# Low parts of MLP tiles behind the next additions, an earlier split of the staged w3, and im0's low part one block ahead

## The chip, the cores and the metric

One core of a Trainium2 chip runs the whole program. The metric is the device time of one execution in microseconds. The engines are TensorE (PE, matmuls), VectorE (DVE), ScalarE (ACT), GpSimd (POOL) and SyncE (SP, which issues every DMA of this kernel). Each engine works through its own list of instructions in order and waits on semaphores for the others.

## What is computed

Two layers, each an FNet mixing block followed by an MLP block, over x of 2048 x 512 in float32. Cut from the reference:

```python
a = einsum("bsd,ed->bse", x, dft_hid_re); b = einsum("bsd,ed->bse", x, dft_hid_im)
y = einsum("ts,bse->bte", dft_seq_re, a) - einsum("ts,bse->bte", dft_seq_im, b)
# MLP block
h = gelu(layernorm(x) @ w1)            # 512 x 512, then quarters of h shifted by +1, -1, +2, -2 rows
x1 = x + shifted(h) @ w2               # 512 x 512
out = x1 + gelu(layernorm(x1) @ w3) @ w4   # 512 x 1376, 1376 x 512
```

Each layer is x + mixing(layernorm(x)), then x + MLP(layernorm(x)).

## The kernel before

Every float32 operand is **split** into a high part (a rounded copy, made by ACT) and a low part (the operand minus the high part, made by DVE, one TENSOR_TENSOR). A product of two operands is three matmuls (`mm3`, lines 283 to 285: high x high, high x low, low x high). So the third matmul of each product needs the low part of the left operand, the second that of the right one. The sequence of 2048 rows is worked on in four chunks of 512.

**Mixing, per chunk.** `x_phase` and `y_phase` build four half products of the sequence transform over eight blocks k each; matrices come from memory by DMA into `raw` tiles, are combined and split into a `ring` of four tiles and used by PE in that order. At the end of `y_phase` the four results (re0, im0, re1, im1, in tiles rr) are split too: `high(im0)` on ACT, `low(im0)` on DVE (line 506, helper line 409). The blocks end in the order (6, by1), (7, by1), (6, by0), (7, by0). In the last chunk the hidden transform (`hid`) follows at once, and its first product reads im0; in the others im0 is read some blocks later in the next chunk. `stream()`, called before each block, emits the splits of the ring tiles that come next, line 246 among them.

**The spatial-shift part.** `by_pairs` runs 32 slots: chunk c has slots 8c to 8c + 7, four `shifted` blocks (x w1, gelu, shift; the result split into tiles rg) and four `mixed` blocks (rg x w2, added to the input on DVE from PSUM, line 688). Other work is hung into these slots by a table: `D(slot, f)` emits f ahead of the slot's own eviction, `A(slot, f)` behind it. There stand the statistics of the next layernorm (`u_stats`), the transposes that turn chunks by way of DRAM (`turn_out` stores a turned chunk, `bring` loads it back), sums of two chunks' blocks (tiles b11 to b22 and t1 to t4, "bt"), and the first loads and splits of w3 and w4.

**The MLP in pairs.** Chunks 0 and 1 (layer 0), and both pairs of chunks (layer 1), go through x w3 two at a time with seven products in place of eight (a scheme of sums and differences of blocks). NF = 11 tiles of 128 hidden units make one single tile and five pairs p = 0 to 4. In layer 0 the w3 pair is loaded raw into one buffer, `staged` (line 869), its four sums are made on DVE (`w3_sums`, line 448, in w3bf), its three groups are split (`w3_highs` on ACT line 887, `w3_lows` on DVE line 893), and the finished w3 is stored to DRAM (`w3_keep`, line 896) for layer 1, which loads it ready made. The w4 tiles are split (`w4_high` line 852, `w4_low` line 856) and stored likewise. There are two w3 buffers (w3b 203 and 205) and six of w4 (w4r).

A pair is, in order of PE: products "11" (bank b1), "t2" (b6), "t1" (b5), "21" (b2), "t3" (b7), then two `w4_part` blocks of the pair before (12 matmuls each, one in p = 0), "t4" (b4) and "22" (b3). A product is six matmuls. The banks come round in fours, so each product overwrites the bank of the fourth one ahead of it: "21" needs "22" of the previous pair to be read, "22" needs "t1" to be read. DVE adds the products up in u, v, x and y (line 448): x and y read the bank of "t1" (b5), x also that of "22". After u and v stand gelu (ACT, line 643, into a tmp tile), the high part (line 646) and the low part (line 647) of h4, which `w4_part` reads a pair later; x and y are kept as gelu in hc and split later. `at_point(0)` to `at_point(5)` emit the preparation of the next pair's weights; `one()` emits one piece of other work from a list (bg), such as `finish` (the layernorm of a chunk) and its transposes. Only layer 0 prepares weights; layer 1 has the pairs with loads alone.

What sets the order of all this is the code's own order: each engine executes its list as written.

## Time and profile before

| | |
|---|---|
| median of 3 runs | 1480.0 us (1479.96 to 1481.51) |
| the profiled execution | 1479.5 us, its span 1477.6 us |
| PE busy | 1455.5 us, 99% of the span |
| DVE busy | 1121.9 us, 76% |
| ACT busy | 715.5 us, 48% |
| DMA | 277 MB, mean 188 GB/s |
| the chain that ended last | PE 80%, DVE 11%, DMA 4%, ACT 2% |

How to read the lines below. Every time is in microseconds from the span's start. A line of the timeline is: start, duration, engine, line of the code, operation, what is written from what, shape, count; in brackets the idle time of the engine before it and what ended that. In a view of waits a line reads: who waits, for whom, the total, the number of times, the longest. A row of stretches gives, after the window, its length and then the busy time (and count) of PE, PE's weight load, DVE, ACT and POOL, the granted PE clock, the share of DMA and its rate in GB/s. A row of DMA issues ends with the size of one and the median time from issue to landing.

### The profile page before, as it was taken

The page shows a single profiled execution, that of the slowest core. Times are in us where ns is not written, and L with a number is a line of the kernel's source. Part 1 is how long each engine was busy: PE and PEld are TensorE (multiplying, and loading weights), DVE is VectorE, ACT ScalarE, POOL GpSimd, SP SyncE. Part 2 cuts the span into 40 slices and gives each one's busy share as a digit, 9 for nine tenths or more (in the row PEclk, how much of TensorE's full clock was granted, in tenths as well). Part 3 has the DMA queues.
Part 4 walks back from the last instruction along what each step waited for, and adds up shares of the span by engine and source line. Part 5 has one row for each costly group of instructions (what it writes and reads, how often), then busy time and mean ns, then how long its engine had stood idle before and what let it go on. Part 6 is the DMA issues. An engine that isn't in the chain of part 4 may idle for free.

```text
span 1477.6 us, 17320 instructions
## 1 busy us (share of the span) xinstructions
PE 1455.5 (99%) x6374; PEld 1190.9 (81%) x6374; DVE 1121.9 (76%) x1558; ACT 715.5 (48%) x953; POOL 86.8 (6%) x111
## 2 busy tenths in 40 slices
PE   9999999999999998999999999999999999999998
PEld 7888888888878776888887888888887788888887
DVE  6876987988868866757989979979888688646443
ACT  5563454444557544435545544644445675333231
POOL 2100000000001000001100000000000010000000
PEclk9999999999999999999999999999999999999999
DMA  6426556566546657862445466565665467768444
GB/s 234 137 87 210 191 187 214 181 196 236 190 127 166 205 176 252 289 208 73 141 130 185 153 204 191 194 219 178 194 225 179 131 166 276 222 213 300 157 133 157
DMA packets 110500, 277.17 MB, mean 188 GB/s; under 512 B 8400, under 2 KB 37072, under 8 KB 108496
## 3 DMA queue, kind: packets, MB, share of 16 engines
q1 hardware_dynamic: 110416, 276.07, 57.1%
q8 instruction: 50, 0.82, 0.2%
q14 instruction: 34, 0.28, 0.1%
HBM read 231.21 MB, written 44.83 MB: 187 GB/s over the span
## 4 chain that ended last, share of the span: by engine, by line
PE 80%; DVE 11%; DMA 4%; ACT 2%; issue 2%; SPq 0%; POOL 0%; DVEq 0%; ACTq 0%
PE psd L285 9%; PE psd L283 8%; PE psd L284 8%; PE psa L283 7%; PE psa L285 7%; PE psa L284 7%; PE psc L285 6%; PE psc L283 6%; PE psc L284 6%; PE psb L285 6%; PE psb L283 6%; PE psb L284 6%; DVE ring L246 2%; DMA raw<-in_ws 2%; DMA staged<-in_w 1%
## 5 line engine op out<-in xcount | busy, mean ns | idle before, releaser
L230 ACT CAST ring<-raw 128x1024 fp32r<-128x1024 f32 (+1 forms) x153 | 156.5, 1029 | 124.2 <-PE psd L285 49.3
L246 DVE TENSOR_TENSOR ring<-raw,ring 128x1024 fp32r<-128x1024 f32 (+1 forms) x153 | 181.7, 1191 | 33.5 <-ACT ring L230 31.5
L283 PE MATMUL psd<-ring,rr 128*128 128x512 f32 x208 | 80.9, 389 | 0.0
L284 PE MATMUL psd<-ring,rr 128*128 128x512 f32 x208 | 80.9, 389 | 0.0
L285 PE MATMUL psd<-ring,rr 128*128 128x512 f32 x208 | 80.9, 389 | 0.0
L647 DVE TENSOR_TENSOR h<-tmp,h 128x512 fp32r<-128x512 f32 x53 | 36.7, 692 | 52.5 <-ACT h L646 50.7
L323 POOL TENSOR_TENSOR rs<-ve,mhalf 128x4 f32<-128x4 f32 x16 | 27.8, 1739 | 612.7 <-DVE nm L322 612.7
L302 POOL TENSOR_TENSOR rs<-ve,mhalf 128x2 f32<-128x2 f32 (+1 forms) x33 | 34.4, 1042 | 423.1 <-DVE nb L301 415.3
L331 ACT ACTIVATE tmp<-xs,nb,rs 128x512 f32<-128x512 f32 x58 | 44.7, 809 | 19.0 <-POOL nb L303 19.0
L284 PE MATMUL psc<-ring,ay 128*128 128x512 f32 x128 | 50.0, 391 | 1.3 <-DVE ring L246 1.2
L237 ACT CAST ring<-ring2f 128x1024 fp32r<-128x1024 f32 x28 | 29.6, 1057 | 44.1 <-DVE ring2f L236 44.1
L283 PE MATMUL psc<-ring,ay 128*128 128x512 f32 x128 | 49.9, 390 | 0.3 <-ACT rr11f L473 0.3
L284 PE MATMUL psb<-ring,ay 128*128 128x512 f32 x128 | 49.9, 390 | 0.2 <-DVE ring L246 0.2
L285 PE MATMUL psc<-ring,ay 128*128 128x512 f32 x128 | 49.8, 389 | 0.0
L285 PE MATMUL psb<-ring,ay 128*128 128x512 f32 x128 | 49.8, 389 | 0.0
L283 PE MATMUL psb<-ring,ay 128*128 128x512 f32 x128 | 49.8, 389 | 0.0
L237 ACT CAST ring<-ring0f 128x1024 fp32r<-128x1024 f32 x28 | 29.6, 1058 | 41.6 <-DVE ring0f L236 41.6
L246 DVE TENSOR_TENSOR ring<-ring1f,ring 128x1024 fp32r<-128x1024 f32 (+1 forms) x50 | 49.2, 983 | 0.6 <-ACT ring L233 0.4
L246 DVE TENSOR_TENSOR ring<-ring3f,ring 128x1024 fp32r<-128x1024 f32 (+1 forms) x50 | 49.1, 982 | 0.2
L285 PE MATMUL psa<-ring,ay 128*128 128x512 f32 x126 | 49.0, 389 | 0.0
L283 PE MATMUL psd<-ring,ay 128*128 128x512 f32 x126 | 49.0, 389 | 0.0
L284 PE MATMUL psa<-ring,ay 128*128 128x512 f32 x126 | 49.0, 389 | 0.0
(480 smaller groups left out, 4369.3 us busy)
## 6 DMA issues: line engine op xcount, KB each, us to landing
raw<-in_ws SPq DMA_DIRECT2D x183, 512.0 KB, 4.9
raw<-in_hs SPq DMA_DIRECT2D x56, 512.0 KB, 3.6
w4r<-w4d SPq DMA_DIRECT2D x55, 512.0 KB, 4.1
w3b<-w3d SPq DMA_DIRECT2D x10, 1792.0 KB, 7.7
raw<-in_w SPq DMA_DIRECT2D x26, 512.0 KB, 3.6
w3d<-w3b SPq DMA_DIRECT2D x5, 1792.0 KB, 6.8
x1d<-tmp SPq DMA_DIRECT2D x12, 512.0 KB, 6.5
xs<-x1d SPq DMA_DIRECT2D x12, 512.0 KB, 6.6
```

The costliest lines, as they stand in the source:

```text
L230: nc.scalar.copy(dest[:, a:b, 0], r[0][:, a:b])
L237: nc.scalar.copy(dest[:, :, 0], lo)
L246: nc.vector.tensor_tensor(lo, src, hi.bitcast(F32), op=ALU.subtract)
L283: nc.tensor.matmul(o, lh, rh, start=first, stop=False)
L284: nc.tensor.matmul(o, lh, rl, start=False, stop=False)
L285: nc.tensor.matmul(o, ll, rh, start=False, stop=last)
L302: nc.gpsimd.tensor_tensor(rs[:, :n], ve[:, :n], mhalf[:, 0, :n], op=ALU.pow)
L323: nc.gpsimd.tensor_tensor(rs, ve, mhalf[:, :, :2], op=ALU.pow)
L331: nc.scalar.activation(o, s, AF.Identity, bias=mr[2], scale=mr[1])
L647: nc.vector.tensor_tensor(dst[:, 1], g, dst[:, 0].bitcast(F32), op=ALU.subtract)
```

## The change

It edits five places, and moves instructions on DVE, ACT and SP; PE's list stays as it was.

1. In `y_phase`, `low(im0)` is emitted before block (6, by0)'s matmuls instead of (7, by0)'s.
2. In each pair of the MLP (both layers), the low part of u's gelu tile goes behind the additions into v and y, that of v's behind the addition of "22" into x.
3. In layer 0's pairs, the low parts of w3's second and third group come at point 2, followed by the load of the next staged w3; the low part of the first group and the store come at point 4; the w4 high parts move to point 3.
4. In layer 0, the first w3 pair is loaded at slot 19, and split in slots 23 to 25 in place of slots 29 to 31 and the start of the MLP; the second is loaded at slot 25. The first low part of w4 is made at slot 31.
5. In layer 0, the statistics `u_stats(2, 2)` move from slot 25 to the list of other work behind the MLP's first block.

```diff
@@ y_phase: the last chunk step for block k == NP - 2, "by0"
-                if last:
+                if k == NP - 2:
                     low(im0)
@@ splitting a gelu tile
+    def split_low(dst, g):
+        nc.vector.tensor_tensor(dst[:, 1], g, dst[:, 0].bitcast(F32), op=ALU.subtract)
+
     def split(dst, g, copy=nc.vector.tensor_copy):
         copy(dst[:, 0], g)
-        nc.vector.tensor_tensor(dst[:, 1], g, dst[:, 0].bitcast(F32), op=ALU.subtract)
+        split_low(dst, g)
+
+    def gelu_high(dst, ps):
+
+        g = tmp_tile()
+        gelu(g, ps)
+        nc.scalar.copy(dst[:, 0], g)
+        return lambda: split_low(dst, g)
@@ by_pairs: the table of slots
-        D(25, u_stats(2, 2))
-
-        A(26, lambda: w3_load(0))
+
         A(28, *[w4_load] * 4)
         if layer == 0:
-            A(29, lambda: w3_highs(0, 1, 2))
-            D(30, lambda: w3_lows(0, 1, 2), lambda: w3_sums(0, 0))
+            A(19, lambda: w3_load(0))
...
             A(30, lambda: w4_high(0), lambda: w4_high(1))
-            D(31, lambda: w3_sums(0, 1))
-            A(31, lambda: w3_highs(0, 0))
+            D(31, lambda: w4_low(0))
         else:
+            A(26, lambda: w3_load(0))
             A(28, lambda: w3_load(1))
+            D(25, u_stats(2, 2))
@@ before the MLP's first block
             if pair == 0:
+                bg += [] if layer else [u_stats(2, 2)]
                 bg += [finish(2, 0), finish(2, 2), turn3(turned, 2, 0, 1), turn3(turned, 2, 2, 3)]
...
             if layer == 0:
-                w4_low(0)
                 w4_low(1)
-                w3_lows(0, 0)
-                w3_keep(0)
-                w3_load(1)
@@ w_prep: what is done at the points of a pair (layer 0)
                     0: [lambda: w3_sums(n, 0), lambda: w3_highs(n, 1, 2)],
                     1: [lambda: w3_sums(n, 1), lambda: w3_highs(n, 0)],
-                    2: [w4_highs],
-                    3: [lambda: w3_lows(n, 0)],
-                    4: [lambda: w3_lows(n, 1, 2), lambda: w3_keep(n), lambda: w3_load(n + 1)],
+                    2: [lambda: w3_lows(n, 1, 2), lambda: w3_load(n + 1)],
+                    3: [w4_highs],
+                    4: [lambda: w3_lows(n, 0), lambda: w3_keep(n)],
                     5: [w4_lows],
@@ the pair
-                gelu_split(h4[2 * (p % 2)], u, act)
+                low1 = gelu_high(h4[2 * (p % 2)], u)
                 at_point(2)
                 prod(b7, w, 2, "t3")
                 add(v, v, b7)
                 add(y, v, b5)
                 gelu(hc[:, 2 * p + 1], y)
                 if layer:
                     one()
+                low1()
                 at_point(3)
...
-                gelu_split(h4[2 * (p % 2) + 1], v, act)
+                low2 = gelu_high(h4[2 * (p % 2) + 1], v)
                 prod(b3, w, 3, "22")
                 add(x, x, b3)
+                low2()
                 gelu(hc[:, 2 * p], x)
```

Lines left out of the table are the rest of the first w3 pair: sums in D(23) and D(24), high parts in A(23) and A(24), all low parts in D(25), the second load in A(25), the store in A(28).

On DVE, in layer 0's pair p = 2 (rest 238 to 241 are u, v, x, y; h 207 the split tile of u's gelu; w3b 205 and w3b1f the next pair's w3; the change's line numbers are up to ten higher for the same statement). Before:

```order
L448 TENSOR_TENSOR w3b1f<-staged 128x256 x2
L448 TENSOR_TENSOR rest_239<-rest_238,psd_249 128x512
L448 TENSOR_TENSOR w3b1f<-w3b1f,staged 128x256
L448 TENSOR_TENSOR w3b1f<-staged,w3b1f 128x256
L448 TENSOR_TENSOR rest_240<-rest_239,psa_242 128x512
L448 TENSOR_TENSOR rest_238<-rest_238,psa_243 128x512
L647 TENSOR_TENSOR h_207<-tmp,h_207 128x512
L448 TENSOR_TENSOR rest_239<-rest_239,psd_248 128x512
L448 TENSOR_TENSOR rest_241<-rest_239,psa_242 128x512
L893 TENSOR_TENSOR w3b_205<-w3b1f,w3b_205 128x1024
L893 TENSOR_TENSOR w3b_205<-staged,w3b_205 128x512
L893 TENSOR_TENSOR w3b_205<-staged,w3b_205 128x256
```

The change, same place:

```order
L448 TENSOR_TENSOR w3b1f<-staged 128x256 x2
L448 TENSOR_TENSOR rest_239<-rest_238,psd_249 128x512
L448 TENSOR_TENSOR w3b1f<-w3b1f,staged 128x256
L448 TENSOR_TENSOR w3b1f<-staged,w3b1f 128x256
L448 TENSOR_TENSOR rest_240<-rest_239,psa_242 128x512
L448 TENSOR_TENSOR rest_238<-rest_238,psa_243 128x512
L903 TENSOR_TENSOR w3b_205<-staged,w3b_205 128x512
L903 TENSOR_TENSOR w3b_205<-staged,w3b_205 128x256
L448 TENSOR_TENSOR rest_239<-rest_239,psd_248 128x512
L448 TENSOR_TENSOR rest_241<-rest_239,psa_242 128x512
L646 TENSOR_TENSOR h_207<-tmp,h_207 128x512
L903 TENSOR_TENSOR w3b_205<-w3b1f,w3b_205 128x1024
```

The two short low parts of w3 moved ahead of the additions into v and y, and h's low part behind them.

On DVE, in layer 0 from slot 22 to slot 27 (tmp is chunk 2's mixed result, b 187 and 189 the split blocks b11 and b21, rg the split result of the shifted blocks). Before, from the eviction of a mixed block on:

```order
L688 TENSOR_TENSOR tmp<-psa_242,tmp 128x512
L409 TENSOR_TENSOR b_189<-b21f,b_189 128x2x512
L647 TENSOR_TENSOR rg_171<-extra_232,rg_171 128x512
L297 BN_STATS st<-tmp 128x6 x2
L299 BN_AGGR mv<-st 128x2 x2
L300 TENSOR_SCALAR ve<-mv 128x2
L301 TENSOR_SCALAR nb<-mv 128x2
L647 TENSOR_TENSOR rg_173<-extra_233,rg_173 128x512
L448 TENSOR_TENSOR bt1f<-b12f,bt1f 128x2x512
L448 TENSOR_TENSOR bt3f<-b22f,b12f 128x2x512
L647 TENSOR_TENSOR rg_172<-extra_232,rg_172 128x512
```

The change, same place:

```order
L409 TENSOR_TENSOR b_187<-b11f,b_187 128x2x512
L448 TENSOR_TENSOR w3b0f<-staged 128x256 x2
L698 TENSOR_TENSOR tmp<-psa_242,tmp 128x512
L409 TENSOR_TENSOR b_189<-b21f,b_189 128x2x512
L448 TENSOR_TENSOR w3b0f<-w3b0f,staged 128x256
L448 TENSOR_TENSOR w3b0f<-staged,w3b0f 128x256
L646 TENSOR_TENSOR rg_171<-extra_232,rg_171 128x512
L903 TENSOR_TENSOR w3b_203<-w3b0f,w3b_203 128x1024
L903 TENSOR_TENSOR w3b_203<-staged,w3b_203 128x512
L903 TENSOR_TENSOR w3b_203<-staged,w3b_203 128x256
L646 TENSOR_TENSOR rg_173<-extra_233,rg_173 128x512
L448 TENSOR_TENSOR bt1f<-b12f,bt1f 128x2x512
```

The sums and low parts of w3's first pair stand where the statistics stood, and ahead of them.

On DVE, at the end of the last chunk's `y_phase` (rr 157 is im0, ring 175 and 177 the first two hidden matrices), the difference of the two orders:

```order
 L448 TENSOR_TENSOR rr11f<-rr00f,rr10f 128x2x512
 L246 TENSOR_TENSOR ring_175<-raw_183,ring_175 128x2x512
+L409 TENSOR_TENSOR rr_157<-rr10f,rr_157 128x2x512
 L246 TENSOR_TENSOR ring_177<-raw_184,ring_177 128x2x512
-L409 TENSOR_TENSOR rr_157<-rr10f,rr_157 128x2x512
 L448 TENSOR_TENSOR rr11f<-rr11f,rr01f 128x2x512
```

im0's low part moved ahead of one low part of a hidden matrix.

## The prediction

> **What bounds the kernel now.** I began with the page's busy times, then asked who waits for whom, with PE as the one that waits.

> ```profile
> PE 1455.5 (99%) x6374; PEld 1190.9 (81%) x6374; DVE 1121.9 (76%) x1558; ACT 715.5 (48%) x953; POOL 86.8 (6%) x111
> ```

> ```profile
> PE psa L283 <- DVE rest L448: 3.8, 4, 1.5
> PE psd L283 <- DVE rest L448: 3.5, 3, 1.7
> PE psd L285 <- DVE w4r L856: 3.2, 1, 3.2
> PE psc L285 <- DVE rr L409: 1.9, 2, 1.4
> ```

> PE is the bound, and the change leaves PE's list of instructions as it was. Time can only come from PE's waits and its clock. The four rows are the waits that end on DVE work the change moves: seven in the MLP for an addition (L448), one for the low part of a w4 tile (L856), two for the low part of im0 (L409). Asked again for 515 to 800 us alone, the view gives the same two L448 rows, so all seven lie in layer 0's five MLP pairs, and layer 1's MLP has none to lose.

> A listed wait is less than what it costs. Twelve matmuls of one block lie between these two starts:

> ```profile
> 499.72 0.39 PE L283 MATMUL psd<-w,rg 128*128 128x512 f32 x1
> 502.44 0.39 PE L283 MATMUL psa<-w,rg 128*128 128x512 f32 x1
> ```

> That is 2.72 / 12 = 0.227 us per matmul, but each is listed as 0.39 us, so a listed wait is 0.16 us short. After a wait the next start follows 0.34 us later, not 0.227, another 0.11:

> ```profile
> 534.48 0.50 PE L283 MATMUL psd<-b,w3b 128*128 128x512 f32 x1 [0.98 <-DVE rest L448]
> 534.82 0.40 PE L284 MATMUL psd<-b,w3b 128*128 128x512 f32 x1
> ```

> So a listed wait w costs w + 0.27 us. For the L856 wait even that is too little; here are its start, the matmul before it, one 13 steps on, and the granted clock (second last but one number of the stretch's row):

> ```profile
> 505.40 0.39 PE L284 MATMUL psd<-b,w4r 128*128 128x512 f32 x1
> 508.97 0.80 PE L285 MATMUL psd<-b,w4r 128*128 128x512 f32 x1 [3.17 <-DVE w4r L856]
> 514.68 0.47 PE L283 MATMUL psd<-b,w4r 128*128 128x512 f32 x1
> 508.00:512.00 4.00, 3.03 (x7) 2.46 (x8) 2.65 (x4) 0.84 (x1) 0.00 (x0) 0.50 0.60 245
> ```

> The waiting matmul was due at 505.40 + 0.23 = 505.63. Thirteen steps later PE should have stood at 505.63 + 13 x 0.227 = 508.58 and stood at 514.68: 6.1 us lost, of which some 2.8 us (13 steps in 5.71 instead of 2.95) because the clock was halved as the gap ended. None of the other waits, up to 1.7 us as listed, is followed by a halved clock.

> [...]

> **The change, part by part. A: im0's low part in the last chunk, both layers.**

> ```profile
> 387.88 2.35 DVE L246 TENSOR_TENSOR ring<-raw,ring 128x1024 fp32r<-128x1024 f32 x2
> 390.15 1.22 DVE L409 TENSOR_TENSOR rr<-rr10f,rr 128x1024 fp32r<-128x1024 f32 x1
> 391.43 0.50 PE L285 MATMUL psc<-ring,rr 128*128 128x512 f32 x1 [0.52 <-DVE rr L409]
> 1131.45 0.50 PE L285 MATMUL psc<-ring,rr 128*128 128x512 f32 x1 [1.35 <-DVE rr L409]
> ```

> The two waits cost 0.52 + 0.27 = 0.79 and 1.35 + 0.27 = 1.62 us. DVE made two low parts of the hidden matrices (2.27 us to the next start, 1.14 each) before im0's. Now im0's stands between them and starts 1.14 us earlier, ending at 390.15 - 1.14 + 1.22 = 390.23. PE wants it at 391.43 - 0.79 + 0.11 = 390.75, so the wait in layer 0 goes: 0.8. In layer 1 the row is late by more, and only the 1.14 us of the shift are won; about 0.4 of wait is left. The second hidden matrix's low part comes 1.14 us later, but it is used one block of 24 matmuls (5.4 us) on. In the other chunks the same swap delays a ring part that PE takes blocks later: nothing. **A = -1.9 us.**

> **B: the pairs of layer 0.** Two waits per pair. The first is at product "22" of one pair, whose bank is wanted by "21" of the next (PE 534.48, above):

> ```profile
> 531.11 0.68 DVE L448 TENSOR_TENSOR rest<-rest,psa 128x512 f32<-128x512 f32 x1
> 531.82 0.63 ACT L643 ACTIVATE tmp<-rest 128x512 f32<-128x512 f32 x1 [4.55 <-DVE rest L448]
> 533.14 0.69 DVE L647 TENSOR_TENSOR h<-tmp,h 128x512 fp32r<-128x512 f32 x1 [1.35 <-ACT h L646]
> 533.75 0.68 DVE L448 TENSOR_TENSOR rest<-rest,psd 128x512 f32<-128x512 f32 x1
> ```

> DVE adds t4 into v, then sits until ACT has made gelu and high part (the low part shows 1.35 us of idle time for it), makes the low part, and only then adds "22" (533.75), which frees the bank. Now that addition follows the first one at once: 531.79 instead of 533.75, before PE wants the bank at 534.48 - 0.98 - 0.16 = 533.34. The second wait is the mirror of it: the addition into y stands behind the other low part.

> ```profile
> 503.38 1.02 DVE L893 TENSOR_TENSOR w3b<-staged,w3b 128x512 fp32r<-128x512 f32 x2
> ...
> 543.08 0.69 DVE L647 TENSOR_TENSOR h<-tmp,h 128x512 fp32r<-128x512 f32 x1 [1.36 <-ACT h L646]
> 544.40 0.69 DVE L448 TENSOR_TENSOR rest<-rest,psa 128x512 f32<-128x512 f32 x1
> 545.14 0.50 PE L283 MATMUL psa<-b,w3b 128*128 128x512 f32 x1 [0.68 <-DVE rest L448]
> ```

> Without the 1.36 us of idle time and the 0.6 us of low part ahead of it, but with two of w3's low parts (1.02 us, the row of 503.38) now there, y is added about 0.9 us sooner, which covers the 0.68 + 0.16 us just barely. So what matters is why DVE was late at all: it stood at the pair's first w3 sum, waiting for the staged w3, behind which v, x, u, v, y all queue.

> ```profile
> 547.71 0.43 SPq L869 DMA_DIRECT2D staged<-in_w  x1
> 555.82 0.76 DVE L448 TENSOR_TENSOR w3b1f<-staged 128x256 f32<-128x256 f32 x2 [4.10 <-DMA staged<-in_w]
> w3d<-w3b SPq DMA_DIRECT2D x4, 1792.0 KB, 6.8
> staged<-in_w SPq DMA_DIRECT2D x3, 512.0 KB, 8.4
> 557.00:575.00 18.00, 15.69 (x68) 12.16 (x67) 10.32 (x19) 6.95 (x13) 0.00 (x0) 1.00 0.83 284
> ```

> The load was issued at the fourth point of the pair, directly behind the 1792 KB store of the finished w3, and landed 8.4 us later (last column); DVE idled 4.1 us. The last row is a pair's stretch with its DMA share and rate. Now the load goes out after the second point and the store after it. Counted from a pair's start T with 6 matmuls per product (1.36 us): "21" ends at 5.5, u is added by 6.2, two w3 lows take 1.0, the load leaves SP at about T + 7.3. The next pair wants it at about T + 15.0 + 1.5, which leaves 9.2 us for a landing that took 8.4 with the store ahead. Then y is added at about T + 8.6 and wanted at T + 13.7; x is added at T + 15.9 and wanted at T + 19.1. Five and three us of slack on DVE; the postponed low parts of h are read by PE one pair later, and the last pair's second one 12 matmuls (2.7 us) behind the pair's end. So all seven waits go: 3.8 + 3.5 + 7 x 0.27 = 9.2. On SP the w4 loads and stores now stand behind the w3 load's wait for DVE; w4 tiles are loaded six ahead, over two pairs. **B = -9.2 us.**

> **C: the start of the MLP.** Splitting w3's first pair moves from the last mixed blocks to six to seven slots earlier, the statistics u_stats(2, 2) go behind the MLP's first block, and w4's first low part goes one addition ahead. From 484.5 to 508.9 DVE had no idle time but 0.2 us, so every insertion shifts all behind it. The rows are the statistics and the low part after them, the last low part of rg and the matmul that takes it, then the moved w3 parts, and w4's low part:

> ```profile
> 488.03 1.27 DVE L297 BATCH_NORM_STATS2 st<-tmp 128x6 f32<-128x512 f32 x2
> 490.00 0.69 DVE L647 TENSOR_TENSOR rg<-extra,rg 128x512 fp32r<-128x512 f32 x1 [0.21 <-ACT rg L646]
> 495.90 0.68 DVE L647 TENSOR_TENSOR rg<-extra,rg 128x512 fp32r<-128x512 f32 x1
> 496.64 0.50 PE L285 MATMUL psa<-w,rg 128*128 128x512 f32 x1
> 504.43 0.76 DVE L448 TENSOR_TENSOR w3b0f<-staged 128x256 f32<-128x256 f32 x2
> 506.84 0.42 DVE L448 TENSOR_TENSOR w3b0f<-w3b0f,staged 128x256 f32<-128x256 f32 x1
> 507.80 1.04 ACT L887 CAST w3b<-w3b0f 128x1024 fp32r<-128x1024 f32 x1 [2.83 <-DVE w3b0f L448]
> 508.23 0.68 DVE L856 TENSOR_TENSOR w4r<-w4r0f,w4r 128x512 fp32r<-128x512 f32 x1
> 509.43 1.22 DVE L893 TENSOR_TENSOR w3b<-w3b0f,w3b 128x1024 fp32r<-128x1024 f32 x1
> ```

> Put in ahead of rg's last low part: sums 0.76 + 2 x 0.42 = 1.6 and lows 1.22 + 1.02 = 2.24, less 0.1 (a start comes about 0.08 before the listed end in front: 508.23 and 509.43 are two instructions apart, 0.60 each); and about 0.5 in which the first low waits for ACT's high part of the sums, 1.04 us long, with only one rg low (0.6) to cover it. Taken out: 490.00 - 488.03 = 1.97. Net +2.3: that low part starts at 495.90 + 2.3 = 498.2 and PE takes it at 498.94 instead of 496.64. This is a **new wait** of about 2.3 us, in two pieces (0.7 at rg's third tile, 1.5 at the last), in a block that loses 0.1 today. Behind the new lows on DVE stand rg's low parts, the bt sums and the evictions of the mixed blocks; behind the new high parts on ACT stand the gelus of the last shifted blocks, with a product block of slack.

> From there to w4's low part it was 12.33 us; lows 1.02, sums 1.6 and one eviction 0.68 (as long as 508.23) less 0.2 of overlap are gone from between: 498.2 + 12.33 - 3.1 = 507.4, done at 508.1, taken by PE at about 508.16 against its own due time of 505.63 + 2.3 = 507.93. A wait of 0.2 us follows, and no gap is long enough to halve the clock. Thirteen steps on PE stands at 508.16 + 0.34 + 12 x 0.227 = 511.22 instead of 514.68. **C = -3.5 us**: DVE gains only 0.8 us here, the rest is the clock. If the clock gate fell all the same, 2.8 of it are lost.

> One condition: the sums write over the buffer from which chunk 1's turned tiles are stored, so DVE waits for that store and for the staged load. SP's next load of those tiles went out when the store had landed:

> ```profile
> 483.13 0.38 SPq L741 DMA_DIRECT2D b12f<-z3d  x1
> ```

> DVE comes to the sums at about 485.7 (488.03 less an eviction, b21's low part and an rg low: 0.60 + 1.13 + 0.60), 2.5 us after that. The load of w3 now stands ahead of that store in the queue, 512 KB more; at the 284 GB/s of the row in B that is 1.8 us, which still fits. [...]

> Sum: 1.9 + 9.2 + 3.5 = **14.6 us**. The profiled execution took 1479.5 us (span 1477.6), the median is 1480.0; I take the sum from the median: **1465.4 us**.

> **Rivals.** *No new wait in C:* if the w3 parts fit into gaps of DVE that I don't see, the whole 6.1 us go: 1480.0 - 1.9 - 9.2 - 6.1 = 1462.8. Against it: DVE shows one idle time of 0.2 us. Chance 0.10. *The clock is halved all the same*, by the two new waits close together: +2.8, 1468.2. For it: the fall of the clock came with a gap; against: single waits up to 1.7 did nothing. 0.08. *Transfers hold the pairs:* the staged load still lands too late, since the same bytes must move in 15 instead of 18 us; the seven waits stay, 1480.0 - 5.4 = 1474.6. Against it: the busiest of the stretches that hold the pairs (557 to 575) moved 284 GB/s at 0.83 of the engines' time, so even its bytes fit in 15 us just about; the others move less. 0.07. *Slower:* DVE, in order, is held at the first w3 sum for turned store and staged load; everything to the MLP's start moves with it one for one, and the clock falls once (2.8). It decides from a hold of 14.6 - 2.8 = 11.8 us, so the store would have to land at 497 instead of 483; a hold of 15 us would give 1480.0 - 14.6 + 2.8 + 15 = 1483.2. 0.02. That the orders aren't moved as said is excluded by the rows of the program's order.

> **Numbers.** The forecast has 0.70, its own range 1464 to 1467 (0.5 us either way in C's waits, 1 us in B's slack). The range of 8 in 10 takes in the first two rivals and a part of the third: 1462.0 to 1470.0. A change of 0.2% (3 us) is about what a measurement of this kernel can tell from none. Everything but the slower rival and 0.03 for what I haven't thought of is faster by more: faster 0.95, same 0.02, slower 0.03.

> **What would show it.** PE's waits for L448 in layer 0 gone, and DVE's wait for staged at the pair's first sum gone (B). No stretch with clock 0.50 near the MLP's start; PE waits there for the low part of rg, 0.7 and 1.5 us, and for w4's low part 0.2 (C). The wait for im0 gone in layer 0 and 0.2 to 0.4 in layer 1 (A). It is wrong if L448 still stands in PE's list, or if a clock below 1.00 shows between 490 and 520 us.

## The result and the profile after

The changed kernel took 1463.1 us as the median of its first four runs (1461.5 to 1466.9) against 1480.0 for the kernel before: a ratio of 0.989, 95% interval [0.9867, 0.9913]. Measured twice more beside other kernels it gave 0.988 [0.9867, 0.9893] and 0.9888 [0.9873, 0.9903]. The forecast was 1465.4 us, 1462.0 to 1470.0. The profiled execution fell from 1479.5 to 1464.26 us, its span from 1477.6 to 1462.5.

The page's busy times, and below them what is left of PE's list of waits where the prediction looked:

```profile
PE 1450.3 (99%) x6374; PEld 1188.7 (81%) x6374; DVE 1122.9 (77%) x1558; ACT 716.9 (49%) x953; POOL 87.3 (6%) x111
```

```profile
PE psa L285 <- DVE rg L646: 1.2, 2, 0.6
...
PE psa L283 <- ACT rg L649: 0.4, 1, 0.4
...
PE psc L285 <- DVE rr L409: 0.2, 1, 0.2
```

No row for an addition (L448) and none for w4r is left. The engines execute as many instructions as before; what is gone is waits and time at half clock. New are the waits at rg (line 646 is the low part that was line 647, 649 the high part).

**The pairs (B).** The stretch that had 97.66 us of PE in 105 (first row, of the kernel before) is now full (second row), and the first sum of a pair starts without waiting for the staged w3, whose load leaves at the second point:

```profile
515.00:620.00 105.00, 97.66 (x418) 77.28 (x417) 70.39 (x123) 45.96 (x75) 3.21 (x4) 1.00 0.70 241
515.00:620.00 105.00, 105.00 (x460) 85.92 (x459) 75.34 (x129) 49.84 (x80) 3.77 (x6) 1.00 0.76 259
```

```profile
515.17 0.75 DVE L448 TENSOR_TENSOR w3b1f<-staged 128x256 f32<-128x256 f32 x2
```

```profile
520.75 0.38 SPq L879 DMA_DIRECT2D staged<-in_w  x1
```

**The start of the MLP (C).** PE's three new waits, the third and the sixteenth matmul of the MLP's first block, and the granted clock of the stretch that stood at 0.50:

```profile
495.56 0.50 PE L285 MATMUL psa<-w,rg 128*128 128x512 f32 x1 [0.55 <-DVE rg L646]
...
497.18 0.50 PE L283 MATMUL psa<-w,rg 128*128 128x512 f32 x1 [0.43 <-ACT rg L649]
...
498.56 0.51 PE L285 MATMUL psa<-w,rg 128*128 128x512 f32 x1 [0.64 <-DVE rg L646]
...
507.77 0.50 PE L285 MATMUL psd<-b,w4r 128*128 128x512 f32 x1
...
510.90 0.39 PE L283 MATMUL psd<-b,w4r 128*128 128x512 f32 x1
```

```profile
508.00:512.00 4.00, 4.00 (x18) 3.24 (x18) 1.23 (x3) 1.22 (x2) 0.00 (x0) 1.00 0.84 283
```

What makes those waits, on DVE and ACT:

```profile
489.74 1.23 DVE L903 TENSOR_TENSOR w3b<-w3b0f,w3b 128x1024 fp32r<-128x1024 f32 x1 [0.52 <-ACT w3b L897]
...
491.00 1.03 DVE L903 TENSOR_TENSOR w3b<-staged,w3b 128x512 fp32r<-128x512 f32 x2
...
494.94 1.05 ACT L406 CAST b<-b12f 128x1024 fp32r<-128x1024 f32 x1 [2.57 <-DVE bt3f L448]
...
495.89 0.59 ACT L643 ACTIVATE extra<-psa 128x512 f32<-128x512 f32 x1
...
496.51 0.62 ACT L649 CAST rg<-extra 128x512 fp32r<-128x512 f32 x1
...
497.82 0.68 DVE L646 TENSOR_TENSOR rg<-extra,rg 128x512 fp32r<-128x512 f32 x1
```

The first two rows are the inserted low parts with the 0.52 us of waiting for ACT. They delay the sum bt3; a high part on ACT waits 2.57 us for that sum, with rg's last gelu and high part queued behind it.

To set executions side by side I take two additions on DVE that read what PE has just finished: the first into xs from psc (L448, in the spatial-shift part of layer 0) and the first one that adds a result of the MLP's pairs (line 1006, now 1021). A row of this view gives, behind the durations, the first and the last start of its group; the first two rows are of the kernel before, the others of the changed one:

```profile
L448 DVE TENSOR_TENSOR xs<-psc,xs x4: 652/664/677, 438.7 to 1179.0; 128x512 f32<-128x512 f32 x4
...
L1006 DVE TENSOR_TENSOR xs<-psc,xs x4: 691/692/692, 602.8 to 1327.7; 128x512 f32<-128x512 f32 x4
```

```profile
L448 DVE TENSOR_TENSOR xs<-psc,xs x4: 651/662/675, 438.6 to 1163.9; 128x512 f32<-128x512 f32 x4
...
L1021 DVE TENSOR_TENSOR xs<-psc,xs x4: 691/692/692, 589.3 to 1312.6; 128x512 f32<-128x512 f32 x4
```

So "the stretch" from 438.7 to 602.8, which holds B and C, took 164.1 us and takes 150.7. In all experiments it can be read the same way. The fourth column is the time in that stretch at a granted clock of 0.50; it belongs to the one profiled execution, the ratio to all runs:

| kernel | first addition | the stretch | of it at half clock | ratio of the times to the kernel before, 95% interval |
|---|---|---|---|---|
| before | 438.7 | 164.1 | 6.8 | 1 |
| A alone | 438.0 | 165.6 | 6.8 | 0.9985 [0.9976, 0.9993] |
| edit 2 alone (low parts) | 439.5 | 159.9 | 0 | 0.9956 [0.9944, 0.9969] |
| edit 3 alone (points) | 438.9 | 156.0 | 3.4 | 0.9957 [0.9943, 0.997] |
| B (2 and 3) | 438.5 | 154.8 | 6.8 | 0.9925 [0.9913, 0.9937] |
| C alone (4 and 5) | 440.2 | 161.4 | 0 | 0.9972 [0.9961, 0.9982] |
| changed, three executions | 438.6, 437.5, 437.9 | 150.7, 151.0, 150.1 | 0 | as above |
| A, B, and w4's low part moved | 438.2 | 155.1 | 3.4 | 0.9915 [0.99, 0.9929] |
| changed, second load late | 438.4 | 150.5 | 0 | 0.9891 [0.9875, 0.9908] |
| changed, rg first | 438.4 | 148.8 | 0 | 0.9883 [0.987, 0.9896] |
| changed, rg first and two moves more | 438.2 | 148.0 | 0 | 0.9882 [0.9868, 0.9897] |

### The profile page after: what moved, and what is told of

It is laid out like the page before. It is cut to its first block, busy times and chain, and to the rows that moved or that the text cites. A ratio compares the mean times of both kernels' runs of the same rounds, so it can differ in the third digit from the quotient of the medians.

```text
span 1462.5 us, 17321 instructions
## 1 busy us (share of the span) xinstructions
PE 1450.3 (99%) x6374; PEld 1188.7 (81%) x6374; DVE 1122.9 (77%) x1558; ACT 716.9 (49%) x953; POOL 87.3 (6%) x111
## 4 chain that ended last, share of the span: by engine, by line
PE 87%; DVE 8%; DMA 2%; ACT 1%; issue 1%; SPq 0%; POOL 0%; DVEq 0%; ACTq 0%
PE psd L285 9%; PE psd L283 9%; PE psd L284 9%; PE psa L283 7%; PE psa L285 7%; PE psa L284 7%; PE psc L285 6%; PE psc L283 6%; PE psc L284 6%; PE psb L285 6%; PE psb L283 6%; PE psb L284 6%; DVE ring L246 2%; DMA raw<-in_ws 1%; DVE st L297 1%
## 5 line engine op out<-in xcount | busy, mean ns | idle before, releaser
L246 DVE TENSOR_TENSOR ring<-raw,ring 128x1024 fp32r<-128x1024 f32 (+1 forms) x153 | 182.0, 1193 | 33.7 <-ACT ring L230 31.7
L283 PE MATMUL psd<-ring,rr 128*128 128x512 f32 x208 | 80.9, 389 | 0.0
L284 PE MATMUL psd<-ring,rr 128*128 128x512 f32 x208 | 80.9, 389 | 0.0
L285 PE MATMUL psd<-ring,rr 128*128 128x512 f32 x208 | 80.9, 389 | 0.0
L284 PE MATMUL psc<-ring,ay 128*128 128x512 f32 x128 | 50.0, 391 | 1.3 <-DVE ring L246 1.3
L283 PE MATMUL psc<-ring,ay 128*128 128x512 f32 x128 | 49.9, 390 | 0.3 <-ACT rr11f L473 0.3
L284 PE MATMUL psb<-ring,ay 128*128 128x512 f32 x128 | 49.9, 390 | 0.0
L285 PE MATMUL psc<-ring,ay 128*128 128x512 f32 x128 | 49.8, 389 | 0.0
L285 PE MATMUL psb<-ring,ay 128*128 128x512 f32 x128 | 49.8, 389 | 0.0
L283 PE MATMUL psb<-ring,ay 128*128 128x512 f32 x128 | 49.8, 389 | 0.0
L246 DVE TENSOR_TENSOR ring<-ring3f,ring 128x1024 fp32r<-128x1024 f32 (+1 forms) x50 | 49.2, 985 | 0.2
L246 DVE TENSOR_TENSOR ring<-ring1f,ring 128x1024 fp32r<-128x1024 f32 (+1 forms) x50 | 49.2, 985 | 0.2
L285 PE MATMUL psa<-ring,ay 128*128 128x512 f32 x126 | 49.0, 389 | 0.0
L284 PE MATMUL psa<-ring,ay 128*128 128x512 f32 x126 | 49.0, 389 | 0.0
L283 PE MATMUL psd<-ring,ay 128*128 128x512 f32 x126 | 49.0, 389 | 0.0
L284 PE MATMUL psd<-ring,ay 128*128 128x512 f32 x126 | 49.0, 389 | 0.0
## 6 DMA issues: line engine op xcount, KB each, us to landing
raw<-in_ws SPq DMA_DIRECT2D x183, 512.0 KB, 4.9
raw<-in_hs SPq DMA_DIRECT2D x56, 512.0 KB, 3.5
w4r<-w4d SPq DMA_DIRECT2D x55, 512.0 KB, 4.0
w3b<-w3d SPq DMA_DIRECT2D x10, 1792.0 KB, 8.2
raw<-in_w SPq DMA_DIRECT2D x26, 512.0 KB, 3.7
w3d<-w3b SPq DMA_DIRECT2D x5, 1792.0 KB, 6.7
x1d<-tmp SPq DMA_DIRECT2D x12, 512.0 KB, 6.6
xs<-x1d SPq DMA_DIRECT2D x12, 512.0 KB, 6.7
```

The costliest lines, as they stand in the source:

```text
L246: nc.vector.tensor_tensor(lo, src, hi.bitcast(F32), op=ALU.subtract)
L283: nc.tensor.matmul(o, lh, rh, start=first, stop=False)
L284: nc.tensor.matmul(o, lh, rl, start=False, stop=False)
L285: nc.tensor.matmul(o, ll, rh, start=False, stop=last)
```

## The experiments

**A alone.** The kernel before with one edit:

```diff
-                if last:
+                if k == NP - 2:
                     low(im0)
```

> The kernel before with only the step of im0's low part (A). My theory: PE's wait for im0's low part goes in layer 0 and shrinks from 1.35 to about 0.2 us in layer 1, nothing takes its place, the time falls by 1.9 us: 1478.1 us against 1480.0. Rival: the second hidden matrix's low part, now 1.1 us later, is waited for instead in both layers; then the two waits only change their name and the time stays at 1480.0.

It took 1478.08 us against 1480.83 (ratio in the table, some 2.2 us). PE's list for im0:

```profile
PE psc L285 <- DVE rr L409: 0.2, 1, 0.2
```

The wait in layer 0 is gone, 0.2 us is left in layer 1, and PE's waits for ring parts (L246), 2.0 us in the kernel before, are 0.9 here, so none took its place: my theory.

**The low parts alone** (edit 2: `gelu_split` becomes `gelu_high`, with `low1()` behind y's addition and `low2()` behind x's).

> The kernel before with only the low parts of the gelu tiles behind the next additions (edit 2, one half of B). Theory 1, the low parts themselves stand in front of the additions PE waits for: the four waits before product 21 (0.98, 0.84, 0.84, 0.85 listed, 4.6 us with 0.27 each) go, and since y is added 1.36 + 0.6 = 1.96 us sooner while it was late by at most 1.67 + 0.16, the three waits before product 22 (0.68, 1.46, 1.67, 4.6 us) go too, although DVE still waits some 4 us for the staged w3: -9.2 us, 1470.8. Theory 2, as the prediction has it for the second kind (the late staged w3 is why DVE is late): the three waits before 22 stay for the most part, -4.6 us, 1475.4.

The median was 1473.58 us, but the profiled execution was the highest of the five (1476.1), so the trace tells which waits are left, not what the median is made of. Of the 4.2 us by which its stretch is shorter, some 2.7 are the clock, which did not fall in it. The four waits before "21" are gone. Two before "22" are left, a third has come in the first pair, one before "t1" as well, and the first low part of the new w3 (L903) is waited for in four pairs; the view below is of DVE, the first of PE:

```profile
526.90 0.50 PE L283 MATMUL psd<-b,w3b 128*128 128x512 f32 x1 [1.02 <-DVE rest L448]
...
529.48 0.50 PE L285 MATMUL psd<-b,w3b 128*128 128x512 f32 x1 [0.47 <-DVE w3b L903]
...
578.34 0.50 PE L283 MATMUL psd<-b,w3b 128*128 128x512 f32 x1 [1.31 <-DVE rest L448]
```

```profile
DVE w3b1f L448 <- DMA staged<-in_w: 10.0, 2, 5.2
DVE w3b0f L448 <- DMA staged<-in_w: 8.5, 2, 5.6
```

Theory 1 falls: with DVE standing 18.5 us at the staged w3, the right order of the low parts doesn't free the banks in time. Theory 2 holds for the waits, but neither foresaw those for w3's own low parts; the median lies between the two forecasts (1470.8 and 1475.4) and decides nothing.

**The points alone** (edit 3: `w3_lows(n, 1, 2)` and the load at point 2, the store behind them at point 4).

> The kernel before with only the new points of the w3 preparation (edit 3, the other half of B). Theory 2 (the late staged w3 makes DVE late): the load is issued some 4 us sooner in the pair, DVE's idle time of 2 to 4 us at the first w3 sum goes, y is added 4.1 - 1.0 = 3.1 us sooner at best and the three waits before product 22 go (-4.6 us); the four waits before 21 stay, since the low part behind v's gelu stands where it stood: 1475.4 us. Theory 1 (only the order of the low parts matters): two w3 low parts, 1.0 us, now stand in front of y's addition, no wait goes, and three grow by up to 1.0 us: 1480 to 1483 us.

1473.05 us. Both kinds of wait are gone but for one each, around the first pair, whose staged w3 still lands late (2.6 us on DVE, second block):

```profile
528.10 0.50 PE L283 MATMUL psd<-b,w3b 128*128 128x512 f32 x1 [1.37 <-DVE rest L448]
...
534.86 0.50 PE L283 MATMUL psd<-b,w3b 128*128 128x512 f32 x1 [0.97 <-DVE rest L448]
```

```profile
DVE w3b1f L448 <- DMA staged<-in_w: 2.6, 1, 2.6
...
DVE w3b0f L448 <- DMA staged<-in_w: 0.3, 1, 0.3
```

Both theories had the waits before "21" staying, since the low part still stands in front of x's addition there. They went: DVE reaches that low part earlier when it hasn't stood at the staged w3. So the late load was a part of both kinds. For the waits before "22" it was the part that counted, since moving the low parts did not remove them; the waits before "21" needed both, the late load and the low part in front, and go with either edit.

**B, both halves**, to see whether they add.

> The kernel before with both halves of B (edits 2 and 3) and nothing else. My theory: all seven waits for the additions go and no wait for w3's low parts takes their place, -9.2 us; less than the two halves give apart (6.5 + 6.4 us), since each alone removes several of the same waits. Rival: the halves add up, -12.9 us, which would need something else than the seven waits.

1470.01 us. No wait for an addition or for w3's low parts is left. The stretch fell by 164.1 - 154.8 = 9.3 us, with the clock halved for 6.8 us at the start of the MLP in both executions: that is the forecast's 9.2, and not the sum of the halves. The ratio says 7.5 thousandths, 11.1 us [9.3, 12.9]; that lies between the two and decides nothing. My theory rests on the trace: the seven waits are gone and the stretch is shorter by their price.

**C alone** (edits 4 and 5).

> The kernel before with only the start of the MLP and the slots changed (edits 4 and 5, C). My theory: the 3.17 us wait for w4's low part and the halved clock behind it go (6.1 us), new waits at rg's low parts cost 2.3 us, and 0.2 is left at w4: -3.5 us, 1476.5. Rival: the clock would have risen by itself in that time or falls again at the new waits: -0.7 us, 1479.3, with a granted clock below 1.00 somewhere between 490 and 520 us.

1476.28 us, 4.1 us [2.7, 5.8] less. The trace has the waits at rg (0.47, 0.43, 0.63 listed), no wait for w4's low part and no clock below 1.00 in the stretch: my theory. Its stretch is only 2.7 us shorter; with the MLP earlier, the pairs in this execution have eight waits for an addition, 7.6 us listed, where the kernel before has seven with 7.3, which is 0.6 us more with 0.27 each.

**Clock: the same gap, five times.** Low parts, points, A and B alone all keep the wait at w4's low part, within 0.04 us of each other as listed, so they show what it does to the clock. Here with the low parts alone: the wait, the next matmul, and the row of the stretch with the granted clock:

```profile
505.99 0.39 PE L284 MATMUL psd<-b,w4r 128*128 128x512 f32 x1
509.51 0.51 PE L285 MATMUL psd<-b,w4r 128*128 128x512 f32 x1 [3.13 <-DVE w4r L866]
509.86 0.39 PE L283 MATMUL psd<-b,w4r 128*128 128x512 f32 x1
```

```profile
508.00:512.00 4.00, 2.49 (x11) 2.05 (x12) 3.19 (x5) 1.04 (x1) 0.00 (x0) 1.00 0.57 228
```

The clock didn't fall at all here. Read in steps of 0.1 us, with the edge inside a step taken from the step's mean, it was at half from 508.00 to 514.83 in the kernel before and from 508.33 to 515.15 with B, but only from 507.86 to 511.28 with A and from 508.56 to 511.98 with the points: 6.8, 6.8, 3.4, 3.4 and 0 us for one and the same gap. Against full speed that lost 2.7 us in the kernel before (14 steps in 6.02 us for 3.29) and 1.5 with A (8 steps in 3.41 for 1.93); in the same way 2.9 with B and 1.4 with the points. In A's execution a wait of 2.02 us in a pair did it too:

```profile
581.74 0.50 PE L283 MATMUL psd<-b,w3b 128*128 128x512 f32 x1 [2.02 <-DVE rest L448]
```

```profile
582.00:583.00 1.00, 1.00 (x5) 0.78 (x5) 0.97 (x2) 0.35 (x1) 0.00 (x0) 0.98 0.00 0
583.00:586.00 3.00, 3.00 (x8) 2.34 (x7) 2.68 (x5) 0.29 (x1) 0.00 (x0) 0.50 0.54 225
```

The clock fell at 582.96, when PE had been at work again for 1.2 us, and rose at 586.37.

**Gaps on purpose.** The changed kernel with a delay on DVE in eight pairs of layer 1:

```diff
                 prod(b3, w, 3, "22")
+                for _ in range((11, 13, 12, 14, 0)[p] if layer and pair == 0 else (12, 13, 11, 14, 0)[p] if layer else 0):
+                    add(y, v, v)
                 add(x, x, b3)
```

> The changed kernel with 11 to 14 additions of 0.6 us, whose result nobody reads, on DVE ahead of the addition of product 22 in eight pairs of layer 1, so that PE stands still some 2.5 to 4.3 us in each. It tells what halves PE's clock. Theory 1, as the prediction had it (length of the gap alone decides, between 1.7 and 3.2 us): every gap above one length halves the clock, for about as long each time and at a fixed delay after PE stops. Theory 2 (a window of about 3.4 us that runs free of the kernel, in which PE must have been idle for most): gaps of the same length halve the clock or not, for one or two windows, and all edges of the clock in this execution lie on one grid of about 3.41 us. The time falls by nothing and rises by the gaps: some 25 us plus 1.7 us for each window at half clock.

The figure of theory 2 stands in the traces above: the spells at half clock lasted 3.41 to 3.42 us (A twice, the points) and 6.82 to 6.83 us (B, the kernel before).

The gaps came out longer than meant, 3.99 to 6.18 us listed, and the time was 1522.5 us in the one run. All eight halved the clock, for 6.8 us five times and 3.4 us three times. Its sixteen edges (fall, rise):

| | | | |
|---|---|---|---|
| 1253.20, 1260.03 | 1277.09, 1283.92 | 1300.99, 1304.40 | 1321.47, 1328.29 |
| 1399.97, 1403.39 | 1420.45, 1427.28 | 1444.35, 1447.76 | 1464.83, 1471.66 |

From the first to the last are 218.46 us, 64 x 3.413, and every edge between lies on that grid within 0.02 us. A's four edges fit as well: 582.96 - 507.86 = 75.10 = 22 x 3.414. So does a third edge of the kernel before, a fall behind its last matmul: 1477.39 - 508.00 = 969.39 = 284 x 3.413. The fall doesn't follow the end of PE's work at a fixed delay: it came 2.3 us after it (1253.20, where PE had last started at 1250.70) at this gap,

```profile
1255.09 0.80 PE L283 MATMUL psd<-b,w3b 128*128 128x512 f32 x1 [4.00 <-DVE rest L448]
```

and 5.0 us after it at the next but one (1300.99, where PE had last started at 1295.72). So theory 2 holds as to the edges: in these executions they lie on a grid of 3.413 us that runs free of PE's stops. How long PE must have stood in a window is told by fewer numbers. In A's pair the clock fell at the end of a window with 2.18 us without work (581.74 - 579.33 - 0.23); in the gap that began at 1295.95 the window that ended at 1297.58 held 1.63 us and kept full clock. If one bound decides, it lies between: an estimate from these two. The execution of the low parts alone fits it. There the clock fell at 1473.94, behind the last matmul; counted back 283 windows of 3.4134 us, an estimate again, an edge lies at 507.9 to 508.0, in the middle of the gap from 506.22 to 509.51, so neither window held more than some 1.75 us without work, and the clock stayed full. At half clock other numbers stand: with 0.24 us without work in the window behind the fall (A, 508.10 - 507.86) and 0.44 (points, 509.00 - 508.56) the clock rose after one window, with 0.67 (B, 509.00 - 508.33) and 0.97 (before, 508.97 - 508.00) it stayed down for a second. Two of the gaps on purpose fit: with 1.89 us (1255.09 - 1253.20) it stayed down for a second, and with none (PE was back at 1300.84, ahead of the fall at 1300.99) it rose after one.

**Only w4's low part moved.** A and B, the slots of the kernel before, and in place of C w4's first low part ahead of the one of t4 in slot 31, with w3's parts behind both:

```diff
+            D(31, lambda: w4_low(0))
...
-            D(30, lambda: w3_lows(0, 1, 2), lambda: w3_sums(0, 0))
...
-            D(31, lambda: w3_sums(0, 1))
+            D(31, lambda: w3_lows(0, 1, 2), lambda: w3_sums(0, 0), lambda: w3_sums(0, 1))
```

> The changed kernel's A and B with the kernel before's slots, and only w4's first low part moved: in slot 31 ahead of t4's low part, with the w3 low parts and sums of slot 30 behind it. My theory: the wait of 3.17 us at the MLP's start and the clock behind it go without the new waits at rg: 2.3 us below the changed kernel, as with the run before this one. Rival: w3's parts, made later by some 2 us, are now waited for in the first pair: at or above the changed kernel.

The rival's time came, 1467.05 us, 4.7 above the changed kernel beside it, but for another reason. The wait at w4 is gone, but DVE then stands 6.27 us at the second staged w3, whose load left behind the 1792 KB store of the first, and PE waits in the first pair. The rows are of SP, DVE and PE:

```profile
510.81 0.33 SPq L906 DMA_DIRECT2D w3d<-w3b  x1
511.18 0.45 SPq L879 DMA_DIRECT2D staged<-in_w  x1
```

```profile
520.08 0.76 DVE L448 TENSOR_TENSOR w3b1f<-staged 128x256 f32<-128x256 f32 x2 [6.27 <-DMA staged<-in_w]
...
526.28 0.68 PE L283 MATMUL psd<-b,w3b 128*128 128x512 f32 x1 [3.14 <-DVE rest L448]
```

The clock was halved for one window behind that, from 526.44 to 529.85.

**The second load late.** To see whether its earlier issue at slot 25 alone is what C needs, the changed kernel with `w3_load(1)` behind `w4_low(1)` again.

> The changed kernel with one move undone: the load of the second staged w3 is issued where the kernel before issued it, at the start of the MLP, and not at slot 25. My theory after the run with w4's low part alone moved: the earlier load is a part of C without which the rest of C is lost, since PE now comes to the first pair 3.8 us sooner and DVE would stand at the staged w3 there: waits of about 1.0 and 3.1 us listed in the first pair, 4.6 us with 0.27 each, and 1.7 us more where a window of the clock falls into the long one: 4 to 6.5 us above the changed kernel beside it. Rival: the load has time enough, and the waits there came from the w3 low parts that stood late on DVE: within 0.5 us of the changed kernel.

1463.23 us, 0.9 above the changed kernel beside it (1462.37), whose own runs reach 1464.1, and far from 4 to 6.5. My theory falls:

```profile
509.54 0.43 SPq L879 DMA_DIRECT2D staged<-in_w  x1
```

```profile
515.91 0.76 DVE L448 TENSOR_TENSOR w3b1f<-staged 128x256 f32<-128x256 f32 x2 [1.01 <-DMA staged<-in_w]
```

DVE waits 1.01 us and PE, for this, not at all. In this kernel the store left at 495.8, as the early split allows, and DVE had the load 6.4 us after its issue; in the run before, behind the store, it took 8.9, left 1.6 us later and was wanted sooner, since PE began the MLP at 504.56 there and not at about 507. So the slot of the load is not what C needs; that the store in front is what makes the difference is argued from these two runs, not tried by itself.

**The changed kernel again, and two with rg first.** The first run changes several things at once: the low parts of w3's second and third group go behind slot 28 and that of the first to slot 31, the load of the second staged w3 to slot 29 and the store to slot 31; w4's high parts go to slot 28, its first low part ahead of slot 30's eviction, and the low parts of t3 and t4 behind w4's second. The other moves also the high part of 12 (A(26) to A(27)) and the sum t4 (D(27) to D(28)), in layer 0.

```diff
-        D(30, lows("t3"))
-        D(31, lows("t4"))
+        if layer:
+            D(30, lows("t3"))
+            D(31, lows("t4"))
...
-            D(25, lambda: w3_lows(0, 0, 1, 2))
-            A(25, lambda: w3_load(1))
-            A(28, lambda: w3_keep(0))
-            A(30, lambda: w4_high(0), lambda: w4_high(1))
-            D(31, lambda: w4_low(0))
+            D(29, lambda: w3_lows(0, 1, 2))
+            A(29, lambda: w3_load(1))
+            A(28, lambda: w4_high(0), lambda: w4_high(1))
+            D(30, lambda: w4_low(0))
+            D(31, lambda: w3_lows(0, 0))
+            A(31, lambda: w3_keep(0))
...
                 w4_low(1)
+                lows("t3")()
+                lows("t4")()
```

> The changed kernel again, beside the next three and on the same chip as they: by its first measurement some 16.5 us below the kernel before (ratio 0.989), by the prediction 14.6. A second profiled execution should show the same waits at rg (0.55, 0.43 and 0.64 us listed) and no wait in the MLP pairs of layer 0.

> The changed kernel, but w3's low parts go behind slot 28, where rg's low parts no longer stand behind them, w4's first low part goes ahead of slot 30's eviction, and the low parts of t3 and t4 go behind w4's second low part. My theory: DVE had the time, only its order was wrong; PE's three waits at rg (0.55, 0.43, 0.64 listed, 2.3 us of delay) go and no wait at w4 comes: 2.3 us below the changed kernel beside it. Rival: DVE has no idle time there, so the wait only moves to w4's low part or to the first products of the pairs: within 0.5 us of the changed kernel.

> The run with rg's low parts first, and two more moves in layer 0: the high part of 12 goes behind the last gelu of chunk 3 on ACT, the sum t4 behind rg's last low part on DVE. My theory: the last wait at rg (0.63 listed, 0.9 us) goes too; in the stretch from the end of the mixing to the end of the first MLP half it takes 148.8 - 0.9 = 147.9 us where the changed kernel takes 150.7 to 151.0, and the time is 2.9 us below the changed kernel beside it. Rival: the earlier run's whole time was level with the changed kernel's because a stretch behind takes the gain back; then this one is level with it as well.

> The changed kernel a third time, beside the two runs before, to compare with them on one chip: 1462.4 us, as in its first eight executions (1461.1 to 1466.9).

The changed kernel came at 1462.38 and 1462.37 us. With rg first one wait at rg is left, 0.63 us,

```profile
496.86 0.50 PE L285 MATMUL psa<-w,rg 128*128 128x512 f32 x1 [0.63 <-DVE rg L646]
```

and with the two moves more, none in the stretch, which takes 148.8 and 148.0 us: 1.3 to 2.2 and 2.1 to 3.0 less than in the three executions of the changed kernel. The times don't show it: 1462.32 and 1461.97 us, within 0.5 us of the changed kernel beside them, with four runs each that spread over 2 to 4 us. So the waits can be had back in the stretch; whether the whole kernel is faster stays open.

## Why the prediction was right, and where not

**A** was forecast at 1.9 us with 0.2 to 0.4 of wait left in layer 1; 0.21 us is left, and A alone gave 2.2 us [1.0, 3.6].

**B** was forecast at 9.2 us; the stretch lost 9.3, the runs 11.1 [9.3, 12.9]. All seven waits are gone, as said. The step that gave each kind its own cause was wrong. I took the wait before "21" for the low part's place and the one before "22" for the late load. The points alone remove all but one wait of each kind; the low parts alone leave some and bring others. The sum held because both edits came together.

**C** was forecast at 3.5 us up to the sixteenth matmul. Counted from the start of chunk 3's mixed blocks, B alone stands there after 514.72 - 494.13 = 20.59 us and the changed kernel after 510.90 - 493.72 = 17.18: 3.4 us. The new wait of "about 2.3 us" at rg was 2.28: the next block started 498.90 - 493.72 = 5.18 us later, where it had been 496.97 - 494.07 = 2.90. The prediction had it in two pieces on DVE; one more is on ACT, which I had not followed behind the sum bt3. So the size of this term came out by some luck. The 0.2 us at w4's low part came (507.33 + 0.23 to 507.77).

The condition on the store held: DVE makes the first sum at 485.34 with no wait. The load that shows the store's landing was issued here,

```profile
483.58 0.38 SPq L751 DMA_DIRECT2D b12f<-z3d  x1
```

10.14 us ahead of the same mixed block where it had been 10.94: 0.8 us later, where 512 KB at 284 GB/s had given 1.8. The 1.8 us was an estimate from size and rate alone, 1.0 us too high here.

**The step that failed in its reason** is the clock: "none of the other waits, up to 1.7 us as listed, is followed by a halved clock" and the row with 0.50 were taken as a rule about length. The runs show edges of the clock on a grid of 3.413 us instead, and one and the same gap (3.13 to 3.17 us listed) followed by 6.8, 6.8, 3.4, 3.4 and 0 us at half clock. The 2.8 us that C counts for the clock were one draw of 2.7, 2.9, 1.5, 1.4 and 0 (five executions with the same gap), so it was luck to take them for the median from one trace. That the sum held all the same has a reason in the runs' clocks: the 36 runs of the kernel before beside these experiments have mean granted clocks of 0.997 to 0.999, 0.9982 on average; of the twelve runs of the changed kernel ten have 1.000 and two 0.999, 0.9998 on average. The difference, 0.0016 of 1478 us, is an estimate of 2.4 us for the clock from these rounded figures. In 21 of the 36 the clock is 0.998 or less. That these lost a window or more on the way is an estimate too: half of 3.41 us is 0.0012 of the span, while the fall behind the last matmul left 0.2 us at half clock in the profiled execution of the kernel before and 0.8 in that of the changed one, 0.0003 at most. A wait in a pair can be such a place, as A's execution shows.

**What the sum missed.** The median fell by 16.9 to 17.9 us, the forecast was 14.6. The medians (1462.4 to 1463.1) lie within 1462.0 to 1470.0 but below the narrower 1464 to 1467. By the number alone the rival without a new wait in C (1462.8) would fit better; the trace excludes it, since the waits at rg are there. The two profiled executions differ by less, 15.1 us of span: 0.1 up to the first addition, 13.4 in the stretch, 1.6 from there to layer 1's first addition into xs from psc (1179.0 - 602.8 = 576.2 before, 1163.9 - 589.3 = 574.6 now), nothing behind it. In the three profiled executions of the changed kernel B and C account for 13.1 to 14.0 in the stretch, where 12.7 were forecast. Outside it the executions differ whatever the edit: 437.5 to 440.2 us to the first addition, and 572.9 to 577.2 between the stretch and layer 1's first addition, where PE's waits for ring parts (L246) come and go. Measured alone, A, B and C gave 2.2, 11.1 and 4.1 us, 17.4 together, so most of what the sum missed came with B. Why is open. Fewer halved windows in the pairs would be a candidate, but the five runs of B alone have a mean clock of 0.998, as the kernel before has.

## What to carry to other kernels

When a chain on an in-order engine is late, look first for the one wait that makes it late: here a load that left late, behind a larger store, had a part in two kinds of waits that each seemed to have a cause of its own. A gain at one place may stand only because another place covers it: with w4's low part moved alone, the late load that the gap had hidden took the gain back (DVE stood 6.27 us at it). And price a halved clock as a chance: in the kernel before no wait of PE up to 1.7 us listed was followed by half clock, those of 2.0 to 3.2 us in the experiments were followed by 6.8 us of it, by 3.4 or by none, and all eight gaps of 3.99 to 6.18 us by 3.4 or 6.8.
